# First products in token blocks of 384 and 512 instead of 448, and loads and splits of pairs issued in other slots

## The chip, the cores and the metric

The kernel runs on one core of one Trainium2 chip. The metric is the device time of one execution in microseconds (us); lower is better. A core has several engines that run side by side: TensorE (PE, matrix products, with weight loads shown as PEld), VectorE (DVE), ScalarE (ACT), GpSimd (POOL), and SyncE (SP), whose queue issues all of this kernel's DMA transfers. The products leave TensorE into PSUM; everything else works from SBUF, and what doesn't fit lies in the chip's DRAM.

## The reference

Eight batches of 448 tokens and twelve heads of 64 columns go through an attention with a sigmoid in place of the softmax; its result goes through a bilinear block of four matrices.

```python
scores = scale * np.matmul(q, k.transpose(0, 1, 3, 2)) - np.log(S)   # (8, 12, 448, 448)
attn = 1.0 / (1.0 + np.exp(-scores))
x = np.matmul(attn, v)           # then reshaped to (3584, 768)
a = x @ w1                       # 768 -> 1024
b = x @ w2
h = a * b @ w3                   # 1024 -> 1024
out = h @ w_out                  # 1024 -> 768
```

The weights are float64 and arrive as pairs of 32-bit words. Inputs q, k, v are float32.

## The kernel before

**Precision.** Most products are made of rounded float32 parts (type F32R): a value is split into a high part (a rounded copy) and a low part (the rest), `split` at L65, and a product of two such values is three matmuls: high by high, high by low, low by high. Weights are decoded from their two words on ACT (`magnitude`, L77) and DVE (`decode`, L82), six DVE instructions from L86 to L102.

**Stages.** The first stage is the attention and, beside it, the first products a and b. The second (L484) multiplies w3 by w_out, 384 columns at a time, and the third (L500) multiplies the stored a*b by the result of that, 512 tokens at a time.

**The attention** goes by pairs of heads: 48 pairs, six per batch (p is the pair's number). The 448 keys of a pair fall into four chunks of 128, 128, 128 and 64, and each chunk is one *slot* of the schedule; the slots are numbered through, pair p has slots 4p to 4p+3. In a slot PE computes the scores of a chunk (`scores`, L189), ACT the sigmoid (`attention`, L202), DVE the low part `al`; one slot later `attend_due` (L366) multiplies by the values (`attend`, L242). With the last chunk, `combine` (L260) turns the pair's result into xh and xl, which are kept per batch: six pairs are the six blocks of 128 columns (kc) of x.

The first nine pairs (`PLAIN = 9`) are computed directly in float32: their q and k are used as loaded. From pair 9 on q, k and v are split: `split_pair` (L151) makes qs and kh on DVE and kl and ks on POOL; `split_v` (L168) makes vs on DVE and POOL. They need a pool (`pf`) that opens at the start of pair 8, when the pool of early weight words is closed.

**Buffers.** The tiles of q and k share three buffers (tag "qk"): a plain pair needs one (q and k side by side), a later pair two. Values vv have two buffers. From weight job 12 on the words `raw` have one. The tile g of a finished block has one as well.

**First products.** `up(b, ...)` (L312) is a generator that issues one matmul per step: for each of 8 blocks fc of the 1024 columns and for w1 and w2, 6 x 3 matmuls with the 448 tokens of batch b as moving operand (L320), 288 in all. Then ACT copies a (L328), DVE multiplies a by b into g (L331) and SP stores g to DRAM (L332). While the attention of batch b+1 runs, 12 of these matmuls are issued in each slot (`take(filler, ups)`), from its third slot on; the last batch's follow behind the attention.

**Weights.** Jobs 0 to 15 are the column blocks of w1 and w2, jobs 16 to 31 the halves of w3. A job is loaded, decoded, and split or stored at slots fixed in `steps`. Around the switch from plain to split pairs, SP gets the load of job 11 in slot 28, of job 12 in slot 31, of job 13 in slot 32, of job 14 in slot 34, of job 15 in slot 35 and of job 16 in slot 38. From job 12 on a load waits until the job before it has been decoded (L102).

**What sets the order.** PE and SP issue in the order of the program text throughout (`manual_schedule`). Until pair 8, ACT and POOL do so too; from there on their order, like DVE's everywhere, is a planner's, fixed when the kernel is built. A DMA that must wait holds up all DMAs behind it in the SP queue. At the start of pair p, before its slots, the text has: load q and k of pair p+2, load v of pair p+1, split v of pair p. At the end of slot 4p+1 it splits q and k of pair p+1.

Of the kernel before, what the change touches and what calls it, by code (L numbers as in the profile page):

```python
# [11 lines left out]
F32 = mybir.dt.float32  # L12
F32R = mybir.dt.float32r
U32 = mybir.dt.uint32
AF = mybir.ActivationFunctionType
ALU = mybir.AluOpType
# [9 lines left out]
def sigmoid_attention_bilinear_ffn(  # L26
# [16 lines left out]
    nc = tc.nc  # L43
    B, H, D, S = qT.shape
    DM, DF = w1.shape[0], w1.shape[1] // 2
    NT = B * S
    P = 128
    CHUNKS = [(c, min(P, S - c)) for c in range(0, S, P)]
    NC = len(CHUNKS)
    assert 2 * D == P and CHUNKS[-1][1] == D  # L50
    NPAIR = H // 2
    NK = DM // P
    NF = DF // P
    NM = DM // 2
    scale = 1.0 / math.sqrt(D)
    PLAIN = 9

    pw = ctx.enter_context(tc.tile_pool(name="pw", bufs=4))
# [1 line left out]
    ps = ctx.enter_context(tc.tile_pool(name="ps", bufs=3, space=PSUM))  # L60
    dram = ctx.enter_context(tc.tile_pool(name="dram", bufs=1, space=bass.MemoryType.DRAM))
    w3_dram = dram.tile([NF, P, NF, P], F32, name="w3_dram")
    g_dram = dram.tile([NF, P, NT], F32, name="g_dram")

    def split(dst_hi, dst_lo, src, hi_engine, lo_engine):  # L65
        hi_engine(out=dst_hi, in_=src)  # L66
        lo_engine.tensor_tensor(out=dst_lo, in0=src, in1=dst_hi, op=ALU.subtract)  # L67
# [40 lines left out]
    pm = phase_x.enter_context(tc.tile_pool(name="pm", bufs=2, side="left"))  # L108
# [3 lines left out]
    px = (px0, px1)  # L112
# [10 lines left out]
    def load_pair(b, hp):  # L123
        heads = slice(2 * hp, 2 * hp + 2)
        if b * NPAIR + hp < PLAIN:

            qk = pa.tile([P, 2, S], F32, name="qp", tag="qk", bufs=3)
            for i, src in enumerate((qT, kT)):
                nc.sync.dma_start(out=qk[:, i], in_=src[b, heads].rearrange("h d s -> (h d) s"))
            return qk[:, 0], qk[:, 1]  # L130
        qq = pa.tile([P, 2, S], F32, name="qq", tag="qk", bufs=3)
        kk = pa.tile([P, 2, S], F32, name="kk", tag="qk", bufs=3)
        for dst, src in ((qq, qT), (kk, kT)):
            for r in range(2):
                nc.sync.dma_start(
                    out=dst[r * D:(r + 1) * D], in_=src[b, heads].rearrange("h d s -> d h s")
                )
        return qq, kk

    def load_v(b, hp):  # L140
        vv = pa.tile([P, NC, 2 * D], F32, name="vv")
        cols = slice(hp * 2 * D, (hp + 1) * 2 * D)
        full = (NC - 1) * P
        nc.sync.dma_start(
            out=vv[:, :NC - 1], in_=v[b, :full, cols].rearrange("(c p) e -> p c e", p=P)
        )
        for r in range(1 if b * NPAIR + hp < PLAIN else 2):
            nc.sync.dma_start(out=vv[r * D:(r + 1) * D, NC - 1], in_=v[b, full:, cols])
        return vv

    def split_pair(plain, qq, kk):  # L151

        if plain:
            return qq, kk, None, None
        qs = pf[0].tile([P, 2, S], F32R, name="qs")
        kh = pf[0].tile([P, 2, S], F32R, name="kh")
        kl = pf[0].tile([P, 2, S], F32R, name="kl")
        nc.vector.tensor_copy(out=qs, in_=qq)
        nc.vector.tensor_tensor(out=qs[D:], in0=qq[D:], in1=qs[D:], op=ALU.subtract)
        split(kh, kl, kk, nc.vector.tensor_copy, nc.gpsimd)  # L160

        ks = pf[0].tile([P, 2, P], F32R, name="ks")
        for j in range(2):
            for i, k in ((j, kh), (1 - j, kl)):
                nc.gpsimd.tensor_copy(out=ks[:, j, i * D:(i + 1) * D], in_=k[:, j, S - D:])
        return qs, kh, kl, ks

    def split_v(plain, vv):  # L168
        if plain:
            return vv  # L170

        vs = pf[0].tile([P, NC, 2, 2, D], F32R, name="vs")
        for j in range(2):
            split(vs[:, :, j, j, :], vs[:, :, j, 1 - j, :], vv[:, :, j * D:(j + 1) * D],
                  nc.vector.tensor_copy, nc.gpsimd)
        return vs
# [5 lines left out]
    def add_halves(dst, src):  # L182

        for j in range(2):
            rows, others = slice(j * D, (j + 1) * D), slice((1 - j) * D, (2 - j) * D)
            nc.scalar.copy(out=dst[rows], in_=src[j][others])  # L186
            nc.vector.tensor_tensor(out=dst[rows], in0=src[j][rows], in1=dst[rows], op=ALU.add)
# [69 lines left out]
                    start=first and m == 0, stop=last and m == len(ops) - 1,  # L257
                )

    def combine(b, accs):  # L260
        xh = px[b % 2].tile([P, S], F32R, name="xh")
        xl = px[b % 2].tile([P, S], F32R, name="xl")
        if len(accs) == 1:
            split(xh, xl, accs[0][:, :S], nc.scalar.copy, nc.vector)
            return xh, xl
        t = pm.tile([P, S], F32, name="t", bufs=1)
        add_halves(t, [acc[:, :S] for acc in accs])
        split(xh, xl, t, nc.scalar.copy, nc.vector)
        return xh, xl

    wh, wl = {}, {}
# [39 lines left out]

    def up(b, xs, banks):  # L312

        for fc in range(NF):
            for n in (1, 2):
                acc = ps.tile([P, 512], F32, name="up", tag=next(banks), bufs=2)
                for kc in range(NK):
                    xh, xl = xs[kc]
                    for m, (w, x) in enumerate(((wh[n], xh), (wh[n], xl), (wl[n], xh))):
                        nc.tensor.matmul(  # L320
                            acc[:, :S], w[:, fc, kc], x,
                            start=(kc == 0 and m == 0), stop=(kc == NK - 1 and m == 2),
                        )
                        if (kc, m) != (NK - 1, 2):
                            yield
                if n == 1:
                    a_sb = pm.tile([P, S], F32, name="a_sb", bufs=1)
                    nc.scalar.copy(out=a_sb, in_=acc[:, :S])  # L328
                    yield
            g = pm.tile([P, S], F32, name="g", bufs=1)  # L330
            nc.vector.tensor_tensor(out=g, in0=acc[:, :S], in1=a_sb, op=ALU.mult)  # L331
            nc.sync.dma_start(out=g_dram[fc, :, b * S:(b + 1) * S], in_=g)  # L332
            yield

    def take(stream, n):
# [7 lines left out]
    pairs = [(b, hp) for b in range(B) for hp in range(NPAIR)]  # L343
# [6 lines left out]

    EARLY = sum(s < (PLAIN - 1) * NC for s in starts)
    qks, vvs = {}, {}
    for p in range(2):
        qks[p] = load_pair(*pairs[p])
        load_job(p)
        if p == 0:
            vvs[0] = load_v(*pairs[0])
    splits, vs = {0: split_pair(0 < PLAIN, *qks.pop(0))}, {}
    weights = decode_weights()
    xs = {b: [] for b in range(B)}  # L360
    filler = iter(())
    waiting = []
    accs = {}
    pf = []

    def attend_due(slot):  # L366
        while waiting and waiting[0][0] <= slot:
            _, p, c, ops = waiting.pop(0)
            if c == 0:
                accs[p] = [  # L370
                    ps.tile([P, 512], F32, name="av", bufs=2) for _ in range(1 if p < PLAIN else 2)
                ]
            attend(c, ops, vs[p], accs[p])
            if c == NC - 2:
                b = pairs[p][0]
                xs[b].append(combine(b, accs.pop(p)))
                del vs[p]

# [3 lines left out]
    for p, (b, hp) in enumerate(pairs):  # L384
        if p == PLAIN - 1:
            order.close()
            order.enter_context(tc.manual_schedule(engines={ET.PE, ET.SP}))
        plain = p < PLAIN
        if p == PLAIN - 1:
            phase_p.close()  # L390
            pf.append(phase_a.enter_context(tc.tile_pool(name="pf", bufs=2, side="right")))
        if p + 2 < len(pairs):
            qks[p + 2] = load_pair(*pairs[p + 2])
        if p + 1 < len(pairs):
            vvs[p + 1] = load_v(*pairs[p + 1])
        vs[p] = split_v(plain, vvs.pop(p))
        qs, kh, kl, ks = splits.pop(p)
        for i, c in enumerate(chunks):
            if not plain and i == 1:
                short = short_scores(ks, qs)  # L400
            else:
                sp = scores(qs, kh, kl, c)
                if not plain and i == 2:
                    waiting.append((slot + 1, p, NC - 1, short_attention(short)))
                waiting.append((slot + 1, p, c, attention(plain, sp)))
            if i == 1 and p + 1 < len(pairs):
                splits[p + 1] = split_pair(p + 1 < PLAIN, *qks.pop(p + 1))
            take(weights, steps.count(slot))
            if b > 0 and (hp, i) == (0, 2):
                take(filler, 10 ** 6)  # L410
                filler = up(b - 1, xs[b - 1], itertools.repeat("up"))
            take(filler, ups)
            attend_due(slot)
            slot += 1
# [22 lines left out]
    for jc in range(NF):  # L437
        take(filler, 10)
        for half in range(2):
            ms = slice(half * NM, (half + 1) * NM)  # L440
            src = w_out[jc * P:(jc + 1) * P].rearrange("p (m u) -> p m u", u=2)[:, ms]
# [33 lines left out]
    for ic in range(NF):  # L475
# [3 lines left out]
        for half in range(2):  # L479
            ms = slice(half * NM, (half + 1) * NM)  # L480
            acc = ps.tile([P, 512], F32, name="up", tag=next(banks), bufs=2)
# [57 lines left out]
```

## Time and profile before

| what | us |
|---|---|
| median of 3 runs | 1111.47 (1111.01 to 1111.79) |
| the profiled execution | 1109.63 |
| its span, first to last instruction | 1107.6 |
| PE busy in the span | 1070.8 |
| DVE busy | 729.3 |
| ACT busy | 563.0 |
| POOL busy | 222.7 |

The profile is one execution. In its views, L12 is line 12 of the kernel; a group is named by what it writes and reads, "up<-xh,w" for instance. Matmuls overlap in the pipeline, so the recorded duration of one (368 ns for 448 columns) is longer than the time from one to the next. The chain of waits goes back from the last instruction and shows what the end waited for, here PE for 87% of the span. SPq is the SP queue: a row stands where a DMA was issued, and a gap before it is a wait. The granted clock is the share of full speed that TensorE was given; its mean over the span is 0.989.

### The profile page before, as it was taken

The numbers are of one execution on the slowest core, as the hardware profiler recorded it, in microseconds if no ns is written. First come the engines' busy times: TensorE is split into PE (matmuls) and PEld (weight loads), VectorE is DVE, ScalarE is ACT, GpSimd is POOL, SyncE is SP. The second block draws the span as 40 slices with busy tenths as digits, with TensorE's granted clock in tenths as the row PEclk, the third lists the DMA queues.
The fourth block names the chain that finished last, engine by engine and source line by source line (L and its number), as shares of the span: only waits on it lengthen the run. The fifth ranks groups of instructions, "written<-read, shape, count | busy, mean of one in ns | idle before, by whom it ended". The sixth has DMA issues, their size and how long they took to land.

```text
span 1107.6 us, 14080 instructions
## 1 busy us (share of the span) xinstructions
PE 1070.8 (97%) x5076; PEld 910.5 (82%) x5076; DVE 729.3 (66%) x1073; ACT 563.0 (51%) x789; POOL 222.7 (20%) x277
## 2 busy tenths in 40 slices
PE   7996959999999999999999999999999999999998
PEld 1253749899899989989889999999999988888887
DVE  6876787788888878888797887857873132122221
ACT  5843647666776767767767776663342111011100
POOL 0001133243343333343333332400000000000000
PEclk9998979999999999999999999999999999999999
DMA  8634365444454434525454343206453021333211
GB/s 257 195 94 125 88 153 148 106 119 111 110 140 128 133 105 122 128 83 136 114 139 129 92 136 86 78 17 201 133 204 109 10 101 71 123 127 130 86 48 47
DMA packets 100692, 129.14 MB, mean 117 GB/s; under 512 B 8016, under 2 KB 82960, under 8 KB 100624
## 3 DMA queue, kind: packets, MB, share of 16 engines
q1 hardware_dynamic: 100624, 128.25, 39.7%
q8 instruction: 40, 0.66, 0.2%
q14 instruction: 28, 0.23, 0.1%
HBM read 98.34 MB, written 29.88 MB: 116 GB/s over the span
## 4 chain that ended last, share of the span: by engine, by line
PE 87%; DVE 6%; DMA 2%; ACT 2%; issue 1%; SPq 1%; POOL 0%; DVEq 0%; POOLq 0%; ACTq 0%
PE up L320 39%; PE up L500 21%; PE av L255 10%; PE sp L199 8%; PE up L484 6%; DMA raw<-w 2%; PE sp L225 1%; PE sp L196 1%; PE av L248 1%; DVE raw L99 1%; DVE f L94 1%; ACT f L79 1%; DVE raw L86 1%; DMA vv<-vL 1%; DVE al L217 1%
## 5 line engine op out<-in xcount | busy, mean ns | idle before, releaser
L320 PE MATMUL up<-xh,w 128*128 128x448 f32 x1536 | 468.2, 368 | 2.3 <-DVE g L331 2.3
L320 PEld LDWEIGHTS up<-xh,w 128*128 128x128 f32 x1536 | 288.9, 188 | 35.7 <-issue 5.3
L320 PE MATMUL up<-xl,w 128*128 128x448 f32 x768 | 281.6, 367 | 0.0
L500 PE MATMUL up<-w 128*128 128x512 f32 x1008 | 228.7, 389 | 0.0
L500 PEld LDWEIGHTS up<-w 128*128 128x128 f32 x1008 | 189.2, 188 | 39.3
L180 ACT ACTIVATE ah<-sp,bias 128x896 fp32r<-128x896 f32 x117 | 117.8, 1006 | 97.2 <-PE sp L199 97.1
L217 DVE TENSOR_TENSOR al<-sp,ah 128x896 fp32r<-128x896 f32 x117 | 127.5, 1090 | 44.2 <-ACT sp L180 42.5
L320 PEld LDWEIGHTS up<-xl,w 128*128 128x128 f32 x768 | 144.5, 188 | 12.9
L67 POOL TENSOR_TENSOR kl<-kk,kh 128x896 fp32r<-128x896 f32 x39 | 104.5, 2678 | 246.4 <-DVE kh L66 195.0
L510 DVE COPY o_sb<-up 128x512 f32<-128x512 f32 x42 | 29.0, 691 | 161.0 <-PE up L500 161.0
L66 ACT CAST w<-graw 128x1024 fp32r<-128x1024 f32 x28 | 29.3, 1055 | 174.7 <-PE up L500 170.5
L67 POOL TENSOR_TENSOR vs<-vv,vs 128x256 fp32r<-128x256 f32 x78 | 67.2, 874 | 251.8 <-DVE vs L66 182.7
L255 PE MATMUL av<-ah,vs 128*128 128x448 f32 x312 | 103.7, 373 | 13.9 <-POOL vs L67 12.7
L180 ACT ACTIVATE sp<-sp,bias 128x896 f32<-128x896 f32 x117 | 113.8, 973 | 0.0
L199 PE MATMUL sp<-qs,kh 128*128 128x448 f32 x234 | 86.3, 369 | 0.0
L199 PE MATMUL sp<-qs,kl 128*128 128x448 f32 x234 | 86.2, 368 | 0.0
L255 PE MATMUL av<-al,vs 128*128 128x448 f32 x234 | 86.2, 368 | 0.0
L239 DVE TENSOR_TENSOR ah<-st,ah 64x448 fp32r<-64x448 f32 x78 | 56.1, 719 | 40.0 <-ACT st L180 38.8
L255 PEld LDWEIGHTS av<-ah,vs 128*128 128x128 f32 x312 | 58.7, 188 | 25.4 <-POOL vs L67 13.7
L79 ACT ACTIVATE f<-raw 128x768 f32<-128x768 f32 (+2 forms) x48 | 34.1, 711 | 64.5 <-DMA raw<-w 28.2
L86 DVE TENSOR_SCALAR raw<-raw 128x768 uint32<-128x768 uint32 (+2 forms) x48 | 35.6, 743 | 38.1 <-ACT f L79 37.9
L186 ACT COPY t<-av 64x448 f32<-64x448 f32 x78 | 41.2, 529 | 34.0 <-PE av L255 33.0
(54 smaller groups left out, 1289.3 us busy)
## 6 DMA issues: line engine op xcount, KB each, us to landing
qq<-qT SPq DMA_DIRECT2D x78, 224.0 KB, 3.6
kk<-kT SPq DMA_DIRECT2D x78, 224.0 KB, 3.8
g_dram<-g SPq DMA_DIRECT2D x64, 224.0 KB, 1.9
graw<-g_dram SPq DMA_DIRECT2D x14, 1024.0 KB, 5.3
raw<-w SPq DMA_DIRECT2D x16, 768.0 KB, 6.2
out<-o_sb SPq DMA_DIRECT2D x42, 256.0 KB, 2.0
vv<-vL SPq DMA_DIRECT2D x48, 192.0 KB, 3.8
raw<-w3T SPq DMA_DIRECT2D x16, 512.0 KB, 4.9
```

What stands on the lines that cost most here:

```text
L67: lo_engine.tensor_tensor(out=dst_lo, in0=src, in1=dst_hi, op=ALU.subtract)
L79: nc.scalar.activation(f, raw[..., 1].bitcast(F32), AF.Abs, scale=HW_SCALE)
L86: nc.vector.tensor_scalar(out=high, in0=high, scalar1=0x80000000, scalar2=0x80000000, op0=ALU.bitwise_and, op1=ALU.bitwise_xor,)
L180: nc.scalar.activation(dst, src, AF.Sigmoid, bias=bias[:n], scale=scale)
L186: nc.scalar.copy(out=dst[rows], in_=src[j][others])
L199: nc.tensor.matmul(sp[:, j], k[:, j, at:at + n], qs[:, j], start=m == 0, stop=m == 1)
L217: nc.vector.tensor_tensor(out=al, in0=sp, in1=ah, op=ALU.subtract)
L239: nc.vector.tensor_tensor(out=a[others, j], in0=t[rows], in1=a[rows, j], op=ALU.subtract)
L255: nc.tensor.matmul(accs[j][:, :S], v[:, c, j].rearrange("p u d -> p (u d)"), a[:, j], start=first and m == 0, stop=last and m == len(ops) - 1,
L320: nc.tensor.matmul(acc[:, :S], w[:, fc, kc], x, start=(kc == 0 and m == 0), stop=(kc == NK - 1 and m == 2),)
L484: nc.tensor.matmul(acc[:, :NM], a[:, jc], w[:, jc, ms], start=(jc == 0 and m == 0), stop=(jc == NF - 1 and m == 2),)
L500: nc.tensor.matmul(acc[:, :TB], w[:, fc, ms], g[:, at, fc % NH], start=(fc == 0 and m == 0), stop=(fc == NF - 1 and m == 2),)
```

## The change

Batches are taken two by two. The first of two passes only its first 384 tokens through its `up`, the second passes 512: the 64 tokens that are left over from the first, and its own 448. The 64 tokens are carried through DRAM, as high and low parts, one piece for each of the six column blocks: stored by `combine` in the first batch, loaded into the front of xh and xl by `combine` in the second.

The loads and splits of pairs move from the start of a pair into its slots, in a function `prepare(p, i)` that runs first in slot i of pair p. Values of a plain pair are loaded in slot 0 of the pair before (now ahead of q and k), those of later ones in slot 1, and split in slot 3 of the pair before instead of at the pair's own start. q and k of plain pairs are still loaded in slot 0 two pairs ahead; those of pairs 9 and 10 in slot 0 of the pair directly before, and their split stands in slot 2 of it; those of pairs from 11 on are loaded in slot 2 two pairs ahead and split in slot 1 of the pair before, at the slot's start instead of its end.

```diff
+    CARRY = 64
+    BLOCKS = (S - CARRY, S + CARRY)
...
+    x_dram = dram.tile([NK, P, 2, CARRY], F32, name="x_dram")
...
-    def combine(b, accs):
-        xh = px[b % 2].tile([P, S], F32R, name="xh")
-        xl = px[b % 2].tile([P, S], F32R, name="xl")
+    def combine(b, kc, accs):
         if len(accs) == 1:
-            split(xh, xl, accs[0][:, :S], nc.scalar.copy, nc.vector)
-            return xh, xl
-        t = pm.tile([P, S], F32, name="t", bufs=1)
-        add_halves(t, [acc[:, :S] for acc in accs])
-        split(xh, xl, t, nc.scalar.copy, nc.vector)
+            src = accs[0][:, :S]
+        else:
+            src = pm.tile([P, S], F32, name="t", bufs=1)
+            add_halves(src, [acc[:, :S] for acc in accs])
+        second = b % 2
+        n = BLOCKS[second]
+        xh = px[second].tile([P, n], F32R, name="xh")
+        xl = px[second].tile([P, n], F32R, name="xl")
+        if second:
+            for i, x in enumerate((xh, xl)):
+                nc.sync.dma_start(out=x[:, :CARRY].bitcast(F32), in_=x_dram[kc, :, i])
+            split(xh[:, CARRY:], xl[:, CARRY:], src, nc.scalar.copy, nc.vector)
+        else:
+            split(xh, xl, src[:, :n], nc.scalar.copy, nc.vector)
+            xt = pm.tile([P, 2, CARRY], F32R, name="xt")
+            split(xt[:, 0], xt[:, 1], src[:, n:], nc.scalar.copy, nc.vector)
+            nc.sync.dma_start(out=x_dram[kc], in_=xt.bitcast(F32))
         return xh, xl
...
     def up(b, xs, banks):
+        n_t = BLOCKS[b % 2]
+        at_t = b // 2 * 2 * S + b % 2 * BLOCKS[0]
...
-                            acc[:, :S], w[:, fc, kc], x,
+                            acc[:, :n_t], w[:, fc, kc], x,
...
-            nc.sync.dma_start(out=g_dram[fc, :, b * S:(b + 1) * S], in_=g)
+            nc.sync.dma_start(out=g_dram[fc, :, at_t:at_t + n_t], in_=g)
...
+    def prepare(p, i):
+        n = p + 1
+        change = n in (PLAIN, PLAIN + 1)
+        if i == (2 if change else 1) and n < len(pairs):
+            splits[n] = split_pair(n < PLAIN, *qks.pop(n))
+        if i == 0 and change:
+            qks[n] = load_pair(*pairs[n])
+        if i == (0 if n < PLAIN else 1) and n < len(pairs):
+            vvs[n] = load_v(*pairs[n])
+        if i == NC - 1 and n < len(pairs):
+            vs[n] = split_v(n < PLAIN, vvs.pop(n))
+        n = p + 2
+        if i == (0 if n < PLAIN else 2) and n not in (PLAIN, PLAIN + 1) and n < len(pairs):
+            qks[n] = load_pair(*pairs[n])
...
-        if p + 2 < len(pairs):
-            qks[p + 2] = load_pair(*pairs[p + 2])
-        if p + 1 < len(pairs):
-            vvs[p + 1] = load_v(*pairs[p + 1])
-        vs[p] = split_v(plain, vvs.pop(p))
         qs, kh, kl, ks = splits.pop(p)
         for i, c in enumerate(chunks):
+            prepare(p, i)
...
-            if i == 1 and p + 1 < len(pairs):
-                splits[p + 1] = split_pair(p + 1 < PLAIN, *qks.pop(p + 1))
             take(weights, steps.count(slot))
```

More of the change, by code (lines that the diff above doesn't have):

```diff
@@ L326, in up @@
                 if n == 1:
-                    a_sb = pm.tile([P, S], F32, name="a_sb", bufs=1)
-                    nc.scalar.copy(out=a_sb, in_=acc[:, :S])
+                    a_sb = pm.tile([P, BLOCKS[1]], F32, name="a_sb", bufs=1)[:, :n_t]
+                    nc.scalar.copy(out=a_sb, in_=acc[:, :n_t])
                     yield
-            g = pm.tile([P, S], F32, name="g", bufs=1)
-            nc.vector.tensor_tensor(out=g, in0=acc[:, :S], in1=a_sb, op=ALU.mult)
-            nc.sync.dma_start(out=g_dram[fc, :, b * S:(b + 1) * S], in_=g)
+            g = pm.tile([P, BLOCKS[1]], F32, name="g", bufs=1)[:, :n_t]
+            nc.vector.tensor_tensor(out=g, in0=acc[:, :n_t], in1=a_sb, op=ALU.mult)
+            nc.sync.dma_start(out=g_dram[fc, :, at_t:at_t + n_t], in_=g)
             yield
@@ L357, in sigmoid_attention_bilinear_ffn @@
             vvs[0] = load_v(*pairs[0])
-    splits, vs = {0: split_pair(0 < PLAIN, *qks.pop(0))}, {}
+    splits, vs = {0: split_pair(0 < PLAIN, *qks.pop(0))}, {0: split_v(0 < PLAIN, vvs.pop(0))}
     weights = decode_weights()
@@ L374, in attend_due @@
             if c == NC - 2:
-                b = pairs[p][0]
-                xs[b].append(combine(b, accs.pop(p)))
+                b, kc = pairs[p]
+                xs[b].append(combine(b, kc, accs.pop(p)))
                 del vs[p]
+    def prepare(p, i):
[12 more added lines that the diff above has]
+            qks[n] = load_pair(*pairs[n])
     chunks = [0, NC - 1, *range(1, NC - 1)]
```

## The prediction

> **What bounds the kernel now.** I read the page first, then the waits of PE, the busy time in stretches of 30 us, and the chain of waits in order of time.
>
> ```profile
> PE 1070.8 (97%) x5076; PEld 910.5 (82%) x5076; DVE 729.3 (66%) x1073; ACT 563.0 (51%) x789; POOL 222.7 (20%) x277
> ```
> ```profile
> PE av L255 <- POOL vs L67: 12.7, 1, 12.7
> PE av L248 <- ACT ap L180: 10.8, 3, 9.1
> ```
> ```profile
> 90.00:120.00 30.00, 26.39 (x108) 15.56 (x109) 23.25 (x30) 14.99 (x19) 9.26 (x12) 0.86 0.34 101
> 120.00:150.00 30.00, 18.16 (x88) 15.97 (x86) 26.75 (x40) 17.73 (x26) 0.43 (x1) 0.88 0.41 108
> ```
>
> The reader sees TensorE at work for 97% of the span, and 22 of the 37 us that are missing in two single waits (12.7 us once, 9.1 us the longest of three). Both lie in these stretches or reach into them, and the granted clock there is 0.86 and 0.88. I call the part from 84 to 157 us the hole. In the second stretch DVE is busier (26.75 of 30 us) than PE (18.16). So there are two prices: the spacing of matmuls outside the hole, and what makes it.
>
> A matmul's recorded duration overlaps the next one, so I take spacings from the chain: length divided by count.
>
> ```profile
> 153.22 2.19 PE av L255 x4
> 155.41 1.42 PE sp L199 x4
> ...
> 187.92 2.44 PE up L320 x12
> ...
> 289.74 2.46 PE up L320 x12
> ...
> 744.28 64.43 PE up L320 x312
> 808.72 66.57 PE up L484 x384
> 875.29 228.54 PE up L500 x1008
> ```
>
> The first products (L320, 448 columns) are spaced 203.3 ns in odd batches, 205.0 in even ones (the rows at 187.92 and 289.74), and 206.5 in the last one (744.28). 384 columns (L484) cost 173.4 ns, 512 columns (L500) 226.7.
>
> The hole is read from the SP queue, and from who waits for it.
>
> ```profile
> 63.91 1.31 SPq L135 DMA_DIRECT2D qq<-qT  x2
> 81.91 1.25 SPq L135 DMA_DIRECT2D kk<-kT  x2
> 83.20 0.59 SPq L144 DMA_DIRECT2D vv<-vL  x1
> 83.85 0.48 SPq L148 DMA_DIRECT2D vv<-vL  x1
> 84.44 0.52 SPq L74 DMA_DIRECT2D raw<-w  x1
> ```
> ```profile
> 111.53 13.15 SPq L74 DMA_DIRECT2D raw<-w  x2
> 124.72 0.54 SPq L332 DMA_DIRECT2D g_dram<-g  x1
> 136.16 0.37 SPq L74 DMA_DIRECT2D raw<-w  x1
> 136.57 1.30 SPq L135 DMA_DIRECT2D qq<-qT  x2
> 137.97 1.25 SPq L135 DMA_DIRECT2D kk<-kT  x2
> ```
> ```profile
> 91.77 0.89 ACT L79 ACTIVATE f<-raw 128x768 f32<-128x768 f32 x1 [17.15 <-DMA raw<-w]
> ```
> ```profile
> 70.97 0.97 PE L248 MATMUL av<-ap,vv 128*64 128x448 f32 x4
> ...
> 79.94 0.97 PE L248 MATMUL av<-ap,vv 64*64 64x448 f32 x4
> ```
>
> SP issues in written order. At 65 us it stands at the keys of pair 9, whose buffer is pair 7's, until 81.91. Behind it wait the values of pair 8 and weight job 11, issued at 84.44. ACT, also in written order then, stands for that job until 91.77, and with it the sigmoids that PE needs: the first wait. After that SP alternates between a weight job and the wait for its single buffer (111.53, 124.3, 136.16); the q and k of pair 11, and behind them the values of pair 10, come only after job 15 at 136.16, so pair 10's values are split late and its attention starts at 153.22: the second.
>
> **The change, part by part.**
>
> *Blocks of 384 and 512.* A pair of batches has 288 matmuls of each. Over four pairs: 288 x (4 x 205.0 + 3 x 203.3 + 206.5 - 4 x (173.4 + 226.7)) ns = 10.4 us less. But batch 0's share runs partly inside the hole. After the slot whose attention begins at 153.22 there remain 96 of its matmuls (96 x 31.6 ns = 3.0 less), three even blocks (288 x 31.6 = 9.1 less each), three odd ones (288 x 23.4 = 6.7 more each) and the last (288 x 20.2 = 5.8 more): together 4.3 us less. The mix of 384 with 448 columns is not shown anywhere; between L484's 173.4 and L320's own 205 I take the former, since L484 keeps it through 384 matmuls.
>
> The Trainium skill ("TensorE: Matmul & The Clock Gate", Back-to-back issue gap) gives an isolated spacing of N/2.4 + 2.5 ns, linear in columns, by which 384 and 512 cost as much as twice 448. The rows differ: 173.4 + 226.7 = 400.1 against 408 to 412.
>
> *The carry.* Loads of its size, and the stream's rate by slices:
>
> ```profile
> GB/s 257 195 94 125 88 153 148 106 119 111 110 140 128 133 105 122 128 83 136 114 139 129 92 136 86 78 17 201 133 204 109 10 101 71 123 127 130 86 48 47
> ...
> vv<-vL SPq DMA_DIRECT2D x87, 32.0 KB, 3.3
> ```
> It adds 24 stores of 64 KB and 48 loads of 32 KB to SP, and on ACT and DVE one 64-column cast and subtract per even pair, while that pair's main split shrinks by 64. Its parts cost below 0.6 us of SP each (rows above) and 3 MB against 129. A carried piece is first read two slots (some 7 us) after its load; loads of that size land in 3.3 us. Cost nothing, covered by that lead; uncovered it would be one wait of some 3 us per odd batch.
>
> *Values before q and k in plain pairs.* Weight jobs now follow 448 KB of q and k that used to be ahead. Job 9 has no slack:
>
> ```profile
> 64.20 0.90 ACT L79 ACTIVATE f<-raw 128x768 f32<-128x768 f32 x1 [3.07 <-DMA raw<-w]
> ```
> Two more issues (0.9 us) and 448 KB at the second slice's 195 GB/s (2.3): 0 to 3.2 us, possibly also at an earlier job. I take 2.5.
>
> *Pair 9's q and k, moved from the start of pair 7 to that of pair 8.* SP no longer stands from 65 to 82. What is late next is pair 8's values, which wait for the attention at 70.97 + 0.97 = 71.9. Three slots of batch 0's product come 1.2 us sooner, the delay above is 2.5, the value loads take 1.2 (83.20 to 84.44): job 11 leaves at **74.4** instead of 84.44.
>
> *Pair 10's q and k, moved from the start of pair 8 to that of pair 9.* This is the edit that costs. In written order they now stand behind jobs 13, 14 and 15, each waiting for the decode before it. Queued behind job 15's wait are also pair 10's values and g stores; pair 10's scores, on PE in written order, wait for the keys.
>
> ```profile
> 103.52 1.09 DVE L159 TENSOR_TENSOR qs<-qq,qs 64x896 fp32r<-64x896 f32 x1
> 104.64 0.96 DVE L102 TENSOR_TENSOR f<-f,raw 128x768 f32<-128x768 f32 x1
> 105.52 0.62 DVE L66 CAST kh<-kk 128x896 fp32r<-128x896 f32 x1
> ```
> ```profile
> 106.27 2.12 POOL L67 TENSOR_TENSOR kl<-kk,kh 128x896 fp32r<-128x896 f32 x1 [105.83 <-DVE kh L66]
> ```
> ```profile
> DMA to landing us min/median/max: 6.3/6.5/6.7
> ```
>
> Job 11's issue to the end of job 12's decode took 105.6 - 84.44 = 21.2 us, of which 1.7 went to pair 9's q (1.09, and a cast that I take at kh's 0.62): 74.4 + 19.5 = 93.9. Job 13's issue to job 15's took 24.6 us: job 15 leaves at **118.5**. Behind it the second key load leaves 2.5 us later (137.97 + 0.63 against 136.16) and lands in 6.6 (the last row shown, of the two key loads of 137.97, which stood behind job 15 too), then kh 0.62 and kl 2.12 with 0.2 of hand-over: 12.0 us, so pair 10's scores can start at **130.5**.
>
> PE gets there sooner. A plain slot takes 4.49 us (two lie between 70.97 and 79.94), now 0.38 less. From 71.9 + 1.3: seven such slots 28.8 us, four of pair 9 (12 products of 173 ns and 4 to 8 others of about 205 to 225 ns) 14.1: **116**. A new wait of 14.5 us replaces both old ones. It also slows the clock: before, the first eight matmuls after the second wait took 3.6 us (the rows at 153.22 and 155.41) instead of 8 x 0.205 = 1.6, a loss of 2.0. I put the same here. The rest of slot 40 and slot 41 up to its attention take 6.2 us: 130.5 + 2 + 6.2 = **138.7** instead of 153.22, 14.5 less; and the 2.0 lost after 153.22 is already paid.
>
> *Splits of pairs and values one slot elsewhere.* Same instructions; the work of DVE is unchanged, and its order is the planner's.
>
> *DVE under shorter slots.* By pair (15.55 us) it alternates with the decode of w3:
>
> ```profile
> 222.20:237.75 15.55, 15.55 (x78) 14.30 (x77) 14.85 (x23) 10.61 (x16) 7.75 (x9) 1.00 0.42 114
> 237.75:253.30 15.55, 15.55 (x78) 14.30 (x77) 11.09 (x17) 10.40 (x16) 5.70 (x8) 1.00 0.49 142
> ```
> (PE, PEld, DVE, ACT, POOL.) A pair beside a 384 block takes PE 48 x 0.1734 + 28 x 0.2055 (the others, 448 columns) = 14.1 us, below DVE's 14.85 where it decodes. Six such pairs lie in batches 3 and 5; hidden by the following light pair at best (0), 1.3 us each at worst (8). I take 0.5 each: 3 more.
>
> **Sum:** -14.5 - 2.0 - 4.3 + 3 = -17.8 us. The profiled execution took 1109.63 us around its span of 1107.6; it gives 1091.8. The median of the runs shown is 1111.47, 1.8 above; on it, **1093.7**.
>
> **The rivals.**
>
> *No new wait at slot 40.* If job 15 left by 104, PE would go through: its attention at 122.3 instead of 138.7, 1077.3. For it: DVE has idle time from 77 to 92 us now. Against: two cycles of 12.3 us lie between jobs 13 and 15, each made of a 5 us load and the decode, and no edit shortens them.
>
> *DVE becomes the bound beside 384 blocks.* All six pairs at 1.3 are 5 more than I put, and as much again from a late order in batch 1: 1104. For it 14.85 against 14.1; against, the pairs between at 11.09.
>
> *The first wait stays.* If job 11 is held up to 84 us by something else in the queue (the values of pair 8, g stores), the change does not do this part: everything after is 10 us later, 1104. Against: pair 6's attention is done at 71.9.
>
> *Spacing linear in columns.* Then 448's 205 ns scale to 175.7 and 234.3; the part after the hole costs 6.7 more instead of 4.3 less: 1105. The three spacing rows speak against. The skill's formula of above is of this kind, and these rows do not bear it out.
>
> *Slower: pair 10 behind a longer chain of jobs.* The decodes of jobs 13 and 14 now meet the attention work of pair 9 on DVE, in an order fixed without knowing the real waits. The total is X + 20.2 - 153.2 - 2.0 - 4.3 + 3, with X the issue of job 15; it exceeds +2.2 us if X passes 138.5, against 118.5 forecast and 136.16 before. At 142 it gives 1117.2. For it: pair 10's keys are needed earlier and after more work than its values were. Against: job 11 leaves ten us sooner.
>
> **How the numbers follow.** Forecast 0.56, with its own range 1087 to 1102; no new wait 0.12; DVE bound 0.10; first wait stays 0.08; linear spacing 0.04; slower 0.10. About 0.2% (2.2 us) is what a measurement of this kernel can tell from no change. Of the first-wait case 0.04 may fall within it; all of the slower one I leave beyond it but 0.01. So faster 0.86, same 0.05, slower 0.09. The range 1080 to 1106 leaves out half of the no-wait case, the slower one and the edges of the others.
>
> **What would show it.** Right: no wait near 84; job 11 issued near 74 and job 15 near 118; PE waiting for kl or kh of pair 10 for some 15 us, near 116 to 131; L320 spaced 173 and 227 ns; few waits on al in batches 3 and 5. Wrong: job 15 near 104 or beyond 136; 384 columns spaced above 180 ns; a PE wait in each decoding pair.

## The result, and the profile after

The changed kernel takes 1123.41 us (median of 4, 1122.29 to 1126.73) against 1111.63 us for the kernel before (median of 4): a ratio of 1.011, 95% interval 1.0087 to 1.0133. It is slower, by about 12 us. The forecast was 1093.7, with a range of 1080 to 1106: wrong in sign.

The page of the changed kernel (span, then busy time of each engine):

```profile
span 1121.8 us, 14296 instructions
...
PE 1077.5 (96%) x5076; PEld 903.8 (81%) x5076; DVE 724.2 (65%) x1097; ACT 566.4 (50%) x813; POOL 186.0 (17%) x277
```

The profiled execution took 1123.74 us. PE's busy time has grown by 6.7 us, although it issues the same 5076 instructions: recorded matmuls get longer at half clock (a scores matmul took 0.57 us instead of 0.37 at 140 us, where the granted clock was 0.50). The two waits of 12.7 and 9.1 us are gone from the list of PE's waits, which is now (engine and line, what it waited for: us in total, times, longest):

```profile
PE av L253 <- ACT ap L185: 7.2, 6, 2.5
PE av L260 <- DVE ah L244: 6.9, 12, 1.8
PE sp L204 <- DVE kh L71: 6.8, 1, 6.8
```

One large wait is left (kh, 6.8), and beside it stand many small ones, for ACT and for DVE. Where the time went is read by stage. The table takes the start of a slot to be its first matmul of scores, from the trace of one execution of each kernel; e1 to e12 are the experiments below. Medians and ratios are of all executions. A ratio is to the kernel before as it was run beside that kernel, and its median then was 1111.6 us for the change, 1112.0 for e1 to e4, 1114.5 for e5 to e8 and 1113.5 for e9 to e12; between these groups ratios compare, medians don't.

| kernel | slots 4 to 26 | 26 to 42 | 42 to the end | median us | ratio (95%) |
|---|---|---|---|---|---|
| before | 42.5 | 96.9 | 952.4 | 1111.6 | 1 |
| after | 49.6 | 84.3 | 972.6 | 1123.4 | 1.011 (1.0087 to 1.0133) |
| e1 | 49.6 | 92.0 | 974.2 | 1134.4 | 1.0199 (1.0175 to 1.0224) |
| e2 | 47.8 | 81.8 | 952.6 | 1098.4 | 0.9882 (0.9852 to 0.9912) |
| e3 | 50.0 | 85.2 | 964.6 | 1120.6 | 1.0076 (1.0052 to 1.0099) |
| e4 | 50.5 | 84.2 | 963.6 | 1116.2 | 1.0041 (1.0018 to 1.0064) |
| e5 | 42.4 | 81.9 | 953.1 | 1094.7 | 0.9825 (0.9796 to 0.9854) |
| e6 | 42.2 | 78.1 | 953.7 | 1092.5 | 0.9808 (0.9784 to 0.9833) |
| e7 | 50.4 | 82.4 | 963.5 | 1117.4 | 1.0029 (1.0014 to 1.0044) |
| e8 | 50.5 | 82.7 | 958.1 | 1110.0 | 0.9969 (0.9954 to 0.9984) |
| e9 | 43.7 | 87.6 | 968.5 | 1118.6 | 1.0044 (1.0031 to 1.0058) |
| e10 | 42.7 | 82.6 | 965.0 | 1110.1 | 0.9967 (0.9948 to 0.9986) |
| e11 | 42.4 | 77.3 | 960.3 | 1099.2 | 0.9868 (0.9851 to 0.9885) |
| e12 | 42.5 | 77.6 | 950.9 | 1090.3 | 0.9787 (0.9772 to 0.9802) |

The part up to slot 4 is left out: slot 4 starts between 14.4 and 18.4 us in these traces, by when four matmuls of a plain slot's scores fall from 1.86 us to 1.02. Against before, the change loses 7.1 us in the early slots, gains 12.6 around the hole, and loses 20.2 from slot 42 on.

**Early slots.** Written order on ACT in the changed kernel (start, duration, instruction, in brackets the idle time before it and what ended it), and DVE beside it:

```profile
43.12 0.82 ACT L71 CAST w<-f 128x768 fp32r<-128x768 f32 x1
43.85 0.48 ACT L71 CAST xh<-av 128x384 fp32r<-128x384 f32 x1
47.46 0.21 ACT L71 CAST xt<-av 128x64 fp32r<-128x64 f32 x1 [3.13 <-DVE xl L72]
47.57 1.00 ACT L185 ACTIVATE ap<-sp,bias 64x896 f32<-64x896 f32 x1
```
```profile
46.00 0.95 DVE L72 TENSOR_TENSOR w<-f,w 128x768 fp32r<-128x768 f32 x1
46.87 0.55 DVE L72 TENSOR_TENSOR xl<-av,xh 128x384 fp32r<-128x384 f32 x1
```

The carried piece's cast takes 0.21 us, but ACT stands 3.13 us ahead of it for DVE's subtract of the main piece, and DVE does that only after the decode of a weight job. The sigmoid queued behind the cast is what PE needs next. (av lies in PSUM: ACT and DVE read there too, not only in SBUF.) The view of the tile xt up to 62 us gives the sum for the first five of batch 0's six pieces:

```profile
its engine sat idle before it (us, times) until:
  DVE xl L72: 8.5, 5
```

**The hole.** The SP queue of the changed kernel:

```profile
78.53 0.53 SPq L79 DMA_DIRECT2D raw<-w  x1
...
100.79 0.39 SPq L79 DMA_DIRECT2D raw<-w  x1
...
112.35 0.39 SPq L79 DMA_DIRECT2D raw<-w  x1
...
124.89 0.37 SPq L79 DMA_DIRECT2D raw<-w  x1
125.31 1.30 SPq L140 DMA_DIRECT2D qq<-qT  x2
126.70 1.25 SPq L140 DMA_DIRECT2D kk<-kT  x2
```

and PE's first scores of pair 10:

```profile
136.86 0.71 PE L204 MATMUL sp<-qs,kh 128*128 128x448 f32 x1 [6.81 <-DVE kh L71]
139.57 0.74 PE L204 MATMUL sp<-qs,kl 128*128 128x448 f32 x1 [2.00 <-POOL kl L72]
```

The rows of raw are weight jobs 11, 13, 14 and 15, and the q and k of pair 10 stand behind the last of them, as forecast.

**From slot 42 on.** TensorE waits there in short pieces for DVE. PE's waits between 160 and 745 us in the changed kernel, and all that the same view lists for the kernel before:

```profile
PE av L260 <- DVE ah L244: 5.7, 10, 1.8
PE sp L204 <- DVE st L192: 3.6, 3, 1.5
PE av L260 <- DVE t L192: 2.3, 4, 0.8
```
```profile
PE av L255 <- DVE t L187: 0.6, 2, 0.5
```

That is 11.6 us against 0.6. What makes DVE late is seen in DVE's and POOL's timelines:

```profile
296.05 0.62 DVE L192 TENSOR_TENSOR st<-sp,st 64x448 f32<-64x448 f32 x1
296.59 2.55 DVE L72 TENSOR_TENSOR xl<-t,xh 128x448 fp32r<-128x448 f32 x1
```
```profile
296.15 2.51 POOL L72 TENSOR_TENSOR kl<-kk,kh 128x896 fp32r<-128x896 f32 x1 [9.60 <-DVE kh L71]
```

(DVE first, POOL second.) The subtract of xl took 2.55 us, where its mean was 0.62 before, and ended 0.48 us behind POOL's kl (299.14 and 298.66). The chain of waits has such a piece on the way to the end (start, us, what):

```profile
322.89 2.51 DVE f L107
325.41 0.18 DVE al L222
...
326.33 0.62 DVE t L192
```

The last step of a decode took 2.51 us there, and the sum t that PE waits for stood behind it.

By batches (from the first slot of one's attention to that of the next) it reads as follows. Batches 2, 4 and 6, beside blocks of 512 columns, take 5.3, 6.5 and 7.3 us more than before. Batches 3 and 5, beside blocks of 384, take 94.1 and 94.7 us against 94.2 and 94.4: the gain that should pay for the others isn't there.

### The profile page after: what moved, and what is told of

It reads as the page before. It is cut to its first block, busy times and chain, and to the rows that moved or that the text cites. A ratio compares the mean times of both kernels' runs of the same rounds, so it can differ in the third digit from the quotient of the medians.

```text
span 1121.8 us, 14296 instructions
## 1 busy us (share of the span) xinstructions
PE 1077.5 (96%) x5076; PEld 903.8 (81%) x5076; DVE 724.2 (65%) x1097; ACT 566.4 (50%) x813; POOL 186.0 (17%) x277
## 4 chain that ended last, share of the span: by engine, by line
PE 79%; DVE 10%; DMA 5%; issue 2%; ACT 2%; SPq 1%; POOL 0%; DVEq 0%; ACTq 0%
PE up L337 34%; PE up L527 20%; PE av L260 8%; PE sp L204 7%; PE up L511 6%; DMA raw<-w 2%; PE av L253 1%; DMA qq<-qT 1%; PE sp L201 1%; DVE f L107 1%; DVE al L222 1%; DMA vv<-vL 1%; PE sp L230 1%; DVE ah L244 1%; DVE raw L104 1%
## 5 line engine op out<-in xcount | busy, mean ns | idle before, releaser
L337 PE MATMUL up<-xh,w 128*128 128x384 f32 (+1 forms) x1536 | 466.5, 367 | 0.0
L337 PE MATMUL up<-xl,w 128*128 128x384 f32 (+1 forms) x768 | 282.3, 368 | 0.0
L72 POOL TENSOR_TENSOR kl<-kk,kh 128x896 fp32r<-128x896 f32 x39 | 87.7, 2250 | 390.8 <-DVE kh L71 325.9
L72 POOL TENSOR_TENSOR vs<-vv,vs 128x256 fp32r<-128x256 f32 x78 | 62.1, 807 | 157.7 <-DVE vs L71 146.0
L244 DVE TENSOR_TENSOR ah<-st,ah 64x448 fp32r<-64x448 f32 x78 | 50.3, 646 | 34.1 <-ACT st L185 32.5
L204 PEld LDWEIGHTS sp<-qs,kh 128*128 128x128 f32 x234 | 44.9, 192 | 18.6 <-issue 13.3
```

The lines of the kernel that those rows point to most:

```text
L204: nc.tensor.matmul(sp[:, j], k[:, j, at:at + n], qs[:, j], start=m == 0, stop=m == 1)
L244: nc.vector.tensor_tensor(out=a[others, j], in0=t[rows], in1=a[rows, j], op=ALU.subtract)
L337: nc.tensor.matmul(acc[:, :n_t], w[:, fc, kc], x, start=(kc == 0 and m == 0), stop=(kc == NK - 1 and m == 2),)
```

## The experiments

**The two halves apart.** e1 keeps blocks and carry on the slots of before; e2 keeps the new slots with 448 tokens in each block and no carry.

```diff
 e1:
+        if p + 2 < len(pairs):
+            qks[p + 2] = load_pair(*pairs[p + 2])
+        if p + 1 < len(pairs):
+            vvs[p + 1] = load_v(*pairs[p + 1])
+        if p:
+            vs[p] = split_v(plain, vvs.pop(p))
...
-            prepare(p, i)
...
+            if i == 1 and p + 1 < len(pairs):
+                splits[p + 1] = split_pair(p + 1 < PLAIN, *qks.pop(p + 1))
 e2:
-    CARRY = 64
+    CARRY = 0
...
```

> The blocks of 384 and 512 with their carry, on the slots of before. Theory: the carry's store stands on SP ahead of the weight jobs of the plain pairs (+6 us by slot 26), the two long waits of before stay, and the shorter slots beside 384 columns make DVE late in batches 3 and 5 (+8 us each): slower than before by some 15 to 25 us, about 1130. Rival: the moved slots cause both losses, and the blocks alone are worth what the spacing gives (2.6 ns on a pair of matmuls, 3 us in all): 1107 to 1111, no loss by slot 26 and none in batches 3 and 5.

> The moved slots alone, every block 448, no carry. Theory: no loss by slot 26, the first long wait is gone and the second is shorter (12 us gained between slots 26 and 42), nothing lost later: about 1099. Rival (values ahead of q and k, and the earlier splits, are at fault): 6 us lost by slot 26, 12 gained in the hole, waits on st and ah in batches 3 and 5 as in the changed kernel: about 1120.

Blocks alone cost 22.4 us, slots alone gain 13.6. Together that would be +8.8; the change measures +11.8. So the gain of the slots is real, and the blocks lose more than one and a half times what they bring. From slot 42 on, e1 has the loss (974.2) and e2 has none (952.6 against 952.4). In e2, though, slots 4 to 26 took 47.8 instead of the 42.5 expected of it: the new order of loads loses there without any carry. Its waits of PE in that stretch and the clock after it:

```profile
PE av L252 <- ACT ap L184: 3.3, 1, 3.3
```
```profile
34.00:36.00 2.00, 2.00 (x8) 0.29 (x4) 1.97 (x3) 0.99 (x2) 0.00 (x0) 0.50 0.58 202
```

(The second row is a stretch of 2 us: busy time of PE, PEld, DVE, ACT and POOL, granted clock, DMA share and rate.) One wait of 3.3 us for sigmoids behind a late weight job is followed by half clock.

**The carry's store, and the place of the splits.** e3 issues the store in the third slot of the next pair, off the way of the loads; e4 puts the splits of pairs from 11 on back at the end of their slot.

```diff
 e3:
-            nc.sync.dma_start(out=x_dram[kc], in_=xt.bitcast(F32))
+            carried.append((kc, xt))
 ...
+            if carried and i == 2:
+                kc, xt = carried.pop()
+                nc.sync.dma_start(out=x_dram[kc], in_=xt.bitcast(F32))
 e4:
-        if i == (2 if change else 1) and n < len(pairs):
+        if i == 2 and change and n < len(pairs):
 ...
+            if i == 1 and p + 1 not in (PLAIN, PLAIN + 1) and p + 1 < len(pairs):
+                splits[p + 1] = split_pair(p + 1 < PLAIN, *qks.pop(p + 1))
             take(weights, steps.count(slot))
```

> The changed kernel with the carry's store issued two slots later, behind the weight job that followed it. If the store's wait on SP is what delays the jobs of the plain pairs, slot 26 starts some 6 us earlier than in the changed kernel (59 instead of 64.9 us), and the total is 1117 or 1118. If the order of values and q, k is at fault, slot 26 stays near 65 us and the total at 1123.

> The changed kernel with the splits of pairs from 11 on back at the end of their slot. If their place ahead of the short scores is what makes st and ah late in batches 3, 5 and 7, these lose 15 us less and the total is about 1108; if the shorter slots beside 384 columns are, it stays between 1119 and 1125.

e3 doesn't mend the early slots (50.0): the store isn't their cause. It is 8.0 us shorter from slot 42 on in its trace, but its interval overlaps that of the change. e4 is 9.0 shorter there and apart from the change by its intervals; it comes out between the two theories. Both only reorder work, so part of the late loss is a matter of order, not of amount; that the order meant is DVE's is read from PE's waits, which all name DVE there.

**Values behind q and k again, then pair 10 ahead of job 15.** Both without blocks: e5 is e2 with the q and k of plain pairs ahead of the values, e6 is e5 with pair 10's q and k issued before job 15's load.

```diff
 e5:
+        if i == 0 and p + 2 < PLAIN:
+            qks[p + 2] = load_pair(*pairs[p + 2])
         if i == (0 if n < PLAIN else 1) and n < len(pairs):
             vvs[n] = load_v(*pairs[n])
 ...
-        if i == (0 if n < PLAIN else 2) and n not in (PLAIN, PLAIN + 1) and n < len(pairs):
+        if i == 2 and n > PLAIN + 1 and n < len(pairs):
 e6:
-        if i == 0 and change:
+        if i == 0 and n == PLAIN:
             qks[n] = load_pair(*pairs[n])
 ...
+            if (p, i) == (PLAIN - 1, NC - 1):
+                qks[p + 2] = load_pair(*pairs[p + 2])
             take(weights, steps.count(slot))
```

> The moved slots alone (448 columns, no carry), with q and k ahead of the values again in the plain pairs. Theory: the values, which wait for PE, hold up q, k and the weight job behind them; with q and k first the plain pairs from slot 4 to slot 26 take 42 to 43 us again as before (47.8 in e2_slots_only), and the total falls from 1098 to about 1093. Rival: the loss there is the phase of the clock at the start and chance in the DMA; then 46 to 48 us and 1098.

> The kernel of e5_qk_first with pair 10's q and k issued in slot 35 ahead of weight job 15. Theory: the wait of pair 10's scores for kh and kl (3.7 us, and half speed behind it) comes from standing behind job 15's wait; it goes, 5 to 6 us below e5_qk_first, about 1087. Rival: the attention of pair 9 is late on DVE anyway and the wait only moves into it: within 2 us of e5_qk_first.

e5 takes slots 4 to 26 back to 42.4: without blocks, the order of values and q, k is the whole loss there. In e6 the queue shows what was meant:

```profile
106.99 1.30 SPq L139 DMA_DIRECT2D qq<-qT  x2
108.34 1.27 SPq L139 DMA_DIRECT2D kk<-kT  x2
118.17 0.37 SPq L78 DMA_DIRECT2D raw<-w  x1
```

and PE no longer waits at slot 40; slots 26 to 42 take 78.1 instead of 81.9. By the medians it is worth 2.2 us, not the 5 to 6 of its theory, and nearer the rival's less than 2. The intervals of the two overlap, but every run of e6 is below every one of e5.

**The early slots with blocks.** e7 is the change with e3's late store and e5's order; it should have mended the early slots if load order and store were their cause. e9 is the change with only the two casts on ACT exchanged and the two subtracts behind both; e10 is e7 with e9's edit.

```diff
-            split(xh, xl, src[:, :n], nc.scalar.copy, nc.vector)
             xt = pm.tile([P, 2, CARRY], F32R, name="xt")
-            split(xt[:, 0], xt[:, 1], src[:, n:], nc.scalar.copy, nc.vector)
+            nc.scalar.copy(out=xt[:, 0], in_=src[:, n:])
+            nc.scalar.copy(out=xh, in_=src[:, :n])
+            for lo, hi, part in ((xl, xh, src[:, :n]), (xt[:, 1], xt[:, 0], src[:, n:])):
+                nc.vector.tensor_tensor(out=lo, in0=part, in1=hi, op=ALU.subtract)
```

> The changed kernel with both, the carry's store two slots later and q and k ahead of the values in plain pairs. Theory: either of the two alone delays the weight jobs by about as much as both, which is why the late store alone gave nothing; with both undone slots 4 to 26 take 43 us (49.6 in the changed kernel) and the total is about 1117. Rival: the additional casts and subtracts of the carry on ACT and DVE delay the plain pairs: 46 us or more, 1120.

> The changed kernel with the carried piece's cast on ACT ahead of xh's, so that ACT, which goes in written order there, doesn't stand for DVE's xl between the two casts (8.5 us in five places of the changed kernel's plain pairs). Theory: this wait is the larger part of the early loss; slots 4 to 26 take 45 to 47 us (49.6 in the changed kernel), the rest being the values ahead of q and k as in e2_slots_only (47.8): total 1119 or 1120. Rival: the carry's store on SP or the DMA traffic is at fault: 49 us and 1123.

> The kernel of e7_plain_repaired (late store, q and k first) with the cast ahead. Theory: nothing of the early loss is left, slots 4 to 26 take 42.5 to 43.5 us (50.5 in e7_plain_repaired), total about 1110. Rival as for e9_cast_first: 49 us or more, 1117.

e7 stayed at 50.4: my theory missed, and the rival (the casts of the carried piece) was left. e9, which changes nothing else, comes to 43.7. Its ACT timeline at the same place has no wait between the casts:

```profile
42.71 0.22 ACT L281 CAST xt<-av 128x64 fp32r<-128x64 f32 x1
42.82 0.50 ACT L282 CAST xh<-av 128x384 fp32r<-128x384 f32 x1
43.23 1.00 ACT L185 ACTIVATE ap<-sp,bias 64x896 f32<-64x896 f32 x1
```

e10 reaches 42.7. By the ratios e9 is some 7 us better than the change (1.0044 and 1.011), and e10 is better than e7 by as much. No run shows why the cast waits for a subtract that reads another part of av; e9 shows that the wait goes with their order.

**DVE's load beside short slots.** e8 is the change without the six DVE instructions that decode each half of w3; its third weight is therefore not the reference's.

```diff
-            f = decode(raws.pop(i), fs.pop(i))
+            f = decode(raws.pop(i), fs.pop(i)) if n < 3 else (raws.pop(i), fs.pop(i))[1]
```

> The changed kernel without the six decode instructions of w3 on DVE (its words are loaded and their scaled magnitude stored, so the third weight is wrong). Theory: beside 384 columns DVE's 15 us per decoding pair don't fit PE's 14.1; without the decode batches 3 and 5 lose nothing and gain what the spacing gives (8 us each instead of 0), and the total is about 1107. Rival: the order on DVE is at fault (splits of pairs ahead of st and ah), and the stalls stay without the decode: 1118 or more.

It comes out between, nearer the theory: 14.5 us less from slot 42 on. Batch 3 (slots 72 to 96) in the change and in e8, columns as above:

```profile
273.00:367.00 94.00, 88.58 (x457) 81.98 (x456) 81.23 (x118) 66.41 (x96) 30.45 (x42) 1.00 0.47 127
```
```profile
272.00:361.00 89.00, 87.89 (x459) 82.62 (x458) 67.66 (x99) 66.41 (x96) 28.16 (x42) 1.00 0.49 127
```

PE does nearly the same work in both, 88.58 and 87.89 us, but needs 94 us for it beside a DVE that is busy for 81.23 and 89 beside one with 67.66. Beside batch 7's attention, where DVE has no w3 to decode (the last decode ended before it), part of the gain of short blocks stays: there the change is 5 us ahead of the kernel before.

**The best of both.** e11 has blocks and carry with all the repairs (e10, e6's move, e4's place of the splits); e12 has the same repairs that apply with 448 tokens and no carry (e6 and e4's place).

> Blocks of 384 and 512 with all that helped: e10_cast_first_plain with pair 10's q and k ahead of job 15 and the splits of later pairs at the end of their slot. Theory: the blocks' spacing (4.6 us in all) is eaten by DVE being late beside 384 columns: 1097 to 1103, not under e6_pair10_early (1092.5). Rival: with the stalls elsewhere gone the spacing shows: 1088 or less.

> e6_pair10_early (448 columns) with the splits of later pairs at the end of their slot. With 448 columns DVE has slack in every batch, so this should change little: 1090 to 1095. If the place of the split ahead of st and ah costs by itself, it gains 3 us or more.

e12 has the lowest time of all, 1090.29 us, 2.1% below the kernel before (ratio 0.9787, 0.9772 to 0.9802; e6's interval overlaps it). Its page and the first of its PE waits:

```profile
span 1088.8 us, 14123 instructions
...
PE 1069.9 (98%) x5076; PEld 910.9 (84%) x5076; DVE 720.2 (66%) x1073; ACT 563.8 (52%) x789; POOL 198.1 (18%) x277
```
```profile
PE sp L200 <- DMA qp<-kT: 4.0, 1, 4.0
PE av L259 <- DVE t L191: 3.0, 3, 1.4
```

No wait above 4.0 us is left, and PE is busy for 98% of the span. With every repair made on both sides, the blocks still cost 8.9 us (1099.2 against 1090.3).

## Why the prediction was wrong, step by step

In the prediction's sum the new slots were to bring 16.5 us (14.5 and 2.0) and the blocks 1.3 (4.3 of spacing, less 3 for DVE). Measured alone, the slots brought 13.6 and the blocks cost 22.4. By stages, the traces of the change and of before differ by +7.1 us in slots 4 to 26 (forecast +2.5), -12.6 up to slot 42 (-19.0) and +20.2 behind it (-1.3). The chain in the hole was read rightly but for one wait; what turned the sign lies in the blocks.

**"Cost nothing" for the carry: failed.** I looked at SP's issues, the traffic and the lead of the loads, which held (no instruction waited for a carried piece), and gave the 64-column cast no price, since the main split shrinks by as much. What counted was its place: on ACT, in written order, behind a wait for DVE and ahead of the sigmoids. ACT lost 8.5 us in five places by it, and e9, which changes only the order of these casts and subtracts, takes slots 4 to 26 from 49.6 to 43.7. The kernel and the trace of before did show both ingredients: ACT in written order until pair 8, and DVE's decode beside it.

**Values ahead of q and k in plain pairs, 0 to 3.2, taken 2.5: too low.** e2 against e5 is 5.4 us, outside the bounds. I priced the later load, not the half clock after the wait that it makes. In e9, which has the same order of loads, the wait was 2.0 us, no half clock followed, and slots 4 to 26 are only 1.0 us longer than e10's with the old order (43.7 and 42.7): it looks as if the price hangs on whether the clock drops.

**Pair 9's q and k; job 11 at 74.4: right in kind.** The wait near 84 is gone. Job 11 left at 78.53; the 4.1 us between are about those lost earlier (6.6 us by slot 26, of which 2.5 were in the forecast).

**Pair 10's q and k behind jobs 13 to 15: right, with a smaller wait, and one ahead of it overlooked.** Job 15 left at 124.89 instead of 118.5, and the first scores of pair 10 came at 136.86, which is 12.0 us behind it, the forecast's distance. PE waited 6.8 + 2.0 us, not 14.5, because it came there late too: at 130.1 us, 14 later than the forecast's 116. Of these 4.2 us were lost before slot 29 and 2.3 in the seven plain slots. The other 7.5 were lost in pair 9's four slots, which I took without a wait:

```profile
120.17 0.71 PE L260 MATMUL av<-ah,vs 128*128 128x448 f32 x1 [3.56 <-DVE xl L72]
```

The granted clock was 0.50 from 120 to 125 us behind it. e6, without blocks, has 4.5 us of such waits at the same place. Slots 26 to 42 gained 12.6 us; the forecast for that stretch, from the same points, was 19.0 (17.8, plus the 2.5 lost before it, less the 1.3 won behind it). e6 shows, in the kernel without blocks, that the wait was due to the place behind job 15.

**Spacing, -4.3 after the hole: a size that was off.** The chain in batch 2, batch 3 and behind the attention:

```profile
252.53 2.75 PE up L337 x12
...
329.20 2.11 PE up L337 x12
...
752.90 69.53 PE up L337 x312
```

Twelve matmuls of 512 columns take 229.2 ns each, twelve of 384 175.8. From all starts in the trace I get 176.7 and 229.0, where I took 173.4 and 226.7 from stages of one size; the last batch alone has 226.7 (288 x 226.7 + 24 x 173.4 ns is 69.5 us). After the hole that is (-28.3 x 960 + 25.7 x 864 + 20.2 x 288) ns, 0.9 us more instead of 4.3 less. A pair of 384 and 512 costs 405.7 ns in the mix against 408.3 for two of 448, so hardly anything was to be had.

**DVE under shorter slots, 0 to 8, taken 3: failed by its size.** From slot 42 on the change is 20.2 us longer than before; less the 0.9 of the spacing, 19.3 are left, of which PE's listed waits for DVE between 160 and 745 us make 11.0 (11.6 less the 0.6 of before). The rest stands in none of these; part of it is a lower clock (0.99 granted from slot 42 to the end of the attention, 1.00 before). I compared DVE's busy time of a pair (14.85) with PE's (14.1) and let the next light pair absorb the rest. e2 and e5, with the same slots and no blocks, have no such loss, and e8, with less work on DVE, keeps 4.8 of it (958.1 - 952.4 - 0.9): so most of it is DVE's work beside the short slots. Order adds to it, as e3 and e4 show, and e11, with the better order, keeps 7.0 (960.3 - 952.4 - 0.9), which would have lain within my bounds. That a DVE instruction grows when it falls beside POOL's was not in the sum at all. By groups between 160 and 745 us (busy us, mean ns), first the change, then before:

```profile
L72 DVE TENSOR_TENSOR xl<-t,xh 128x448 fp32r<-128x448 f32 x19 | 21.2, 1117 | 0.6 <-ACT xh L71 0.4
```
```profile
L67 DVE TENSOR_TENSOR xl<-t,xh 128x448 fp32r<-128x448 f32 x37 | 23.0, 621 | 0.0
...
L86 DVE TENSOR_SCALAR raw<-raw 128x512 uint32<-128x512 uint32 x15 | 19.6, 1304 | 0.0
```

Before, POOL's work stretched the first step of a decode (1304 ns, 422 in the change; the long ones ended some 0.3 us behind a kl), which nothing waits for at once; now it stretches the subtract of x, with the attention of the next slot behind it. But this isn't what the loss mainly comes from. The same group in e1, e4 and e8, in this order:

```profile
L72 DVE TENSOR_TENSOR xl<-t,xh 128x448 fp32r<-128x448 f32 x18 | 11.2, 621 | 0.0
L72 DVE TENSOR_TENSOR xl<-t,xh 128x448 fp32r<-128x448 f32 x19 | 11.7, 616 | 0.0
L72 DVE TENSOR_TENSOR xl<-t,xh 128x448 fp32r<-128x448 f32 x20 | 19.3, 964 | 2.8 <-ACT xh L71 2.6
```

e1 has the whole loss from slot 42 on (974.2) and no stretched subtract, e4 keeps 10.3 us of it (963.6 - 952.4 - 0.9) without one, and e8 has them and keeps only 4.8. No run takes away the stretch alone, so its own share stays open.

**The rivals.** "DVE becomes the bound beside 384 blocks" was the right mechanism. Its price was 5 us more in batches 3 and 5 and 5 more in batch 1; from slot 42 on some 16 came. "Linear spacing" gives 175.7 and 234.3 ns: near the mix for 384 columns, too long for 512. "Slower" was given for another cause, a job 15 later than 138.5; it left at 124.89. The sign came from two steps that I had at 0 and 3.

## What to carry to other kernels

An added instruction is priced by its place in its engine's order, with what it must wait for and what stands behind it: each cast took 0.21 us, and together they cost 6. Time taken from PE in a slot is a gain only while every engine that must finish within the slot keeps room, so compare each engine's period with the new slot, with its slowest recorded durations and not its mean ones. When a change has two halves, run each alone first: here the better half alone beats both kernels.

## What the runs showed of the hardware

**Half clock after short waits.** In the change PE waited 1.73 us at 21.65 and got this (2-us stretches, columns as above):

```profile
20.00:22.00 2.00, 0.35 (x2) 0.19 (x4) 1.97 (x5) 1.51 (x3) 0.00 (x0) 1.00 0.77 232
22.00:24.00 2.00, 2.00 (x8) 0.50 (x4) 1.97 (x3) 1.22 (x2) 0.00 (x0) 0.64 1.02 322
24.00:26.00 2.00, 2.00 (x6) 0.29 (x4) 1.25 (x2) 1.01 (x1) 0.00 (x0) 0.50 1.03 345
```

A wait of 2.51 us at 48.62 was followed by 0.50 as well, e2's 3.3 us by the half clock of its row above, but 2.00 us in e9 by none (1.00 throughout). So the length alone doesn't decide. The Trainium skill ("TensorE: Matmul & The Clock Gate", Why this matters for your kernels) advises no gaps of PE above about 3 us; here 1.73 already brought half clock once.

**DVE beside POOL.** A subtract of 128x448 with both inputs in SBUF (xl) took 2.55 us while POOL's kl of 2.51 us ran, against a mean of 0.62 before. Just ahead of it the addition st, which reads one input from PSUM, took 0.62 us although kl had begun. The Trainium skill ("SBUF — State Buffer", SBUF: two separate sides) says that GpSimd and a DVE instruction with two SBUF inputs lock each other out of a shared port pair for a whole instruction; the trace agrees with it.

**Spacing in a mix.** Behind matmuls of 448 columns the first five of twelve with 512 stood 228 to 236 ns apart and the rest 226.7; those with 384 lay between 174 and 180. The cause stays open.
